# Attention on one Trainium2 core: another order of score and maxima tiles within two steps

## The chip, the cores and the metric

The kernel runs on one core of one Trainium2 chip. TensorE (PE in the profile) multiplies, VectorE (DVE) and ScalarE (ACT) read the results out of PSUM, GpSimd (POOL) works on SBUF alone, SyncE (SP) and POOL issue most DMAs. The metric is device time in microseconds (us) for one execution, a median of several.

## The reference, cut to what matters

A transformer block with adaptive layer norm: softmax attention over 2048 tokens with 32 heads of 18 features, then a gated feed-forward layer (576 to 4608 and back). The change touches the attention alone.

```python
mod = (_silu(c) @ w_mod).reshape(c.shape[0], 6, 1, -1)
h = _layernorm(x) * (1 + ca) + sa
q, k, v = qkv[0], qkv[1], qkv[2]                 # B=1, S=2048, D=576, H=32, Dh=18
scores = jnp.einsum("bhqd,bhkd->bhqk", q, k) * scale
p = _softmax(scores, axis=-1)
o = jnp.einsum("bhqk,bhkd->bhqd", p, v)
x = x + ga * (o @ wo)
h = _layernorm(x) * (1 + cb) + sb
x = x + gb * ((_sigmoid(h @ w_gate) * (h @ w_up)) @ w_down)
```

## The kernel before, in words

Attention is cut into 32 units `u`: a half of the queries (1024) and a pair of heads. A unit has 16 steps `kt`, one for each 128 keys. A step computes four **score tiles** (letter `t`, L1055): 128 keys by 512 queries, for the two heads `h` and the two query chunks `c`. ACT turns each into probabilities with an exponential (L1059, tiles `p0` to `p3`). Two steps later these are multiplied with the values (`values`, L629) and summed in one PSUM tile `o`, which collects a whole unit.

The exponential needs the maximum of each row of scores. So beside unit `u` the maxima for a later unit are found: a step also computes four **maxima tiles** (letter `m`, L524, generator `maxima`), 128 queries by 512 keys, in the order of the table `MAXIMA` or `MAXIMA_H`. DVE reduces seven of eight of them (L530; the one with `h == 0, kc == 1` in L535, together with `over`). The eighth (`h == 0, kc == 0`) is read by ACT, which writes it to `over` (L533); `over` has one buffer.

Scores and maxima use only half of TensorE's rows (56 and 54 of 128): head 0 the upper half, head 1 the lower one. So two neighbouring products of different heads run beside each other as a **pair**. The values product takes four column groups at once.

Every product of either kind, and every transpose, takes the next of seven PSUM banks in turn (`bank()`, tiles `s0` to `s6`). A product can start only when the reader of the seventh allocation before it is done.

Two steps, an even and an odd one, make a **double step**. The order within it is written out by hand as a string for each, and TensorE and ACT keep that order (manual schedule). In most double steps ("halved") the values of the odd step are split in two calls of 256 columns. I call the full call `v`, the two halves `a` and `b`, and number the 16 products of a halved double step 0 to 15. The other letters place the work that comes once in a while:

- `s` and `c`: the maxima of a unit are turned into rows: a transpose on TensorE (L555, in `spread`), a copy on ACT (L559) and a subtraction on DVE (L560). It happens at `kt` 12 of a unit.
- `k` (`taken`): at the end of a unit ACT copies the finished `o` to `oT` (L646). `o` has one buffer, so the next unit's first `v` waits for that copy. It happens at `kt` 1 of the next unit, behind `b`.
- `w` and `c` at `kt` 3 (`outputs`): four transposes of `oT` (L656) into one bank, a reciprocal on DVE (L661), a copy on ACT (L672) that frees the bank.

From step 240 on, rows of the output projection and of the second layer norm (transposes L743, L760, L886, products L776) come in as well, and double steps with L776 aren't halved.

Of the kernel before, what the change touches and what calls it, by code (L numbers as in the profile page):

```python
# [47 lines left out]

MAXIMA = ((1, 0), (0, 0), (1, 1), (0, 2), (1, 2), (0, 3), (0, 1), (1, 3))
SINGLE = (0, 1)  # L50
MAXIMA_H = ((1, 0), (0, 0), (1, 1), (0, 2), (0, 3), (1, 2), (0, 1), (1, 3))
SIDES_H = ((1, 0), (1, 1), (0, 1), (0, 0))
SIDES = ((0, 0), (0, 1), (1, 0), (1, 1))
ORDERED = 7
SEVENS = NB - 2
# [6 lines left out]
def tile_block(ctx, tc, x_in, wqkv, wo, w_gate, w_up, w_down, c_in, w_mod, out):  # L62
# [26 lines left out]
    def bank():  # L89

        turns["bank"] += 1
        return ps[turns["bank"] % 7].tile([P, 512], F32, name=f"s{turns['bank'] % 7}")
# [281 lines left out]
    with tc.tile_pool(name="ln", bufs=2) as ln:  # L374
# [31 lines left out]
        order = ExitStack()  # L406
# [68 lines left out]
    def heads(u):  # L475
        return qsets[u % 3], ksets[u if u < 2 else 2 + (u - 2) % 3]

    def load_heads(u):


        qs, ks = heads(u)
        half, p = divmod(u, H // 2)
        n = S if u < 2 else S + 512
        own = slice(half * HW, (half + 1) * HW)
        for h in range(2):
            rows = slice((2 * p + h) * DH, (2 * p + h + 1) * DH)
            two, one = (slice(64 * h + a, 64 * h + b) for a, b in ((0, 2 * DH), (2 * DH, 3 * DH)))
            nc.sync.dma_start(
                qs[two, :].bitcast(F32), qd[:, rows, own].rearrange("l f n -> f l n").bitcast(F32)
            )  # L490
            nc.sync.dma_start(qs[one, :].bitcast(F32), qd[0, rows, own].bitcast(F32))
            nc.sync.dma_start(
                ks[two, 0:n].bitcast(F32),
                kd[0, rows, 0:n].unsqueeze(1).to_broadcast([DH, 2, n]).bitcast(F32),
            )
            nc.sync.dma_start(ks[one, 0:n].bitcast(F32), kd[1, rows, 0:n].bitcast(F32))
# [3 lines left out]
    def maxima():  # L500
# [4 lines left out]
        for u in range(UNITS):  # L505
# [4 lines left out]
            for i in range(8 * n):  # L510
# [7 lines left out]
                pairs = u not in SINGLE  # L518
                h, kc = (MAXIMA_H if state.get("halved") else MAXIMA)[i % 8]
                rows = slice(64 * h, 64 * h + 3 * DH)  # L520
# [30 lines left out]
    def spread(qs, nm):  # L551

        n = HW // P
        tp = bank()[0 : 2 * n, 0:P]
        nc.tensor.transpose(tp, nm.rearrange("p h t -> p (h t)"), ident)  # L555
        yield
        mrows = small.tile([32 + 2 * n, P], F32R, name="mrows", bufs=1)
        parts = [mrows[32 * l : 32 * l + 2 * n] for l in range(2)]
        nc.scalar.copy(parts[0], tp)  # L559
        nc.vector.tensor_sub(parts[1], tp, parts[0].bitcast(F32))  # L560
        for h in range(2):
            for l, part in enumerate(parts):
                to = 64 * h + 3 * DH + l
                nc.sync.dma_start(
                    qs[to : to + 1, :].rearrange("l (t q) -> l t q", q=P).bitcast(F32),
                    part[n * h : n * (h + 1), :].bitcast(F32),
                )
# [4 lines left out]
    def turn():  # L572
        if turns["s"] < turns["to"]:
            turns["s"] += 1
            next(todo, None)
# [65 lines left out]
    def taken():  # L641

        if "whole" in state:
            half, p, acc = state.pop("whole")
            oT = epool.tile([P, 512], F32, name="oT")
            nc.scalar.copy(oT, acc)  # L646
            state["end"] = (half, p, oT)
# [350 lines left out]
    def load_x(n, name=None):  # L998
        if name:
            X[n] = slots.tile([P, 5, 512], F32R, name=name)  # L1000
        nc.gpsimd.dma_start(X[n], xs[0, n])
# [8 lines left out]
    for u in range(UNITS):  # L1010
        half, p = divmod(u, H // 2)
        qs, ks = heads(u)
        if 0 < u < UNITS - 2:
            load_heads(u + 2)
        if u == H // 2:
            Os.append(big.tile([P, 8, 640], F32, name="big"))
        for kt in range(NT):
            step = u * NT + kt
            turns["to"] = 64 + 4 * LEAD + 4 * (step + 1)
            kcols = slice(kt * P, (kt + 1) * P)  # L1020
            if kt % 2 == 0:
                heavy = state.get("next") == "g"
                hold = heavy and (kt == 2 or kt == 12 and u < UNITS - 1)
                state["halved"] = step >= 10 and (hold or not heavy)
            halved = state["halved"]
            sides = iter(SIDES_H if halved else SIDES)
            probs = [None] * 4
            order = ("vmmtmmtsactt", "wmcmbkttmtmt") if halved else ("vtmmttmvtm", "ktmwttmctmm")
            for does in order[kt % 2]:
                if does == "m":  # L1030
                    turn()
                elif does == "k":
                    taken()
                elif does in "ws":
                    if kt == 3:
                        follow.append(outputs())
                        next(follow[-1], None)
                    if "spread" in state and halved == (does == "s"):
                        follow.append(spread(*state.pop("spread")))
                        next(follow[-1])  # L1040
                    if step >= FROM0 and not hold and halved == (does == "s"):
                        state["next"] = next(rows0 if step < FROM1 else rows1, None)
                elif does == "c":
                    while follow:
                        next(follow.pop(0), None)
                elif does == "v":
                    if step >= LAG:
                        values()
                elif does in "ab":
                    values(slice(0, 256) if does == "a" else slice(256, 512))  # L1050
                else:
                    c, h = next(sides)
                    sT = bank()
                    rows = slice(64 * h, 64 * h + 3 * DH + 2)
                    nc.tensor.matmul(  # L1055
                        sT, ks[rows, kcols], qs[rows, c * 512 : (c + 1) * 512], start=True, stop=True
                    )
                    pr = probs[2 * c + h] = ppool.tile([P, 512], F32, name=f"p{2 * c + h}")
                    state["exp"] = nc.scalar.activation(pr, sT, AF.Exp, scale=SCALE)  # L1059
            pending.append((half, p, kt, probs))  # L1060
            if u in (1, 3):
                if kt == 0:
                    a = big.tile([P, 8, 640], F32, name="big")
                    a = a.rearrange("p a b -> p (a b)")[:, 0 : 8 * D].rearrange("p (t c) -> p t c", t=4)
                    b = slots.tile([P, 2560], F32, name="w0")[:, 0 : 2 * D]
                    mods = load_mod(a, b, 1 + u // 2)
                    row = slots.tile([P, 2560], F32, name="w1")[:, 0:544]
                    weighed = weigh(mods)
                elif kt >= 5:
                    next(weighed, None)  # L1070
            elif u in (2, 4) and kt in (2, 4):
                takes = [(ga_b, None), (mcol2[:, 1, :], 0.0)] if u == 2 else [(mcol2[:, 0, :], 1.0), (gb_b, None)]
                if kt == 2:
                    weighed = modulate(row, mods[:1], HALVES, takes)
                next(weighed, None)
            if 4 * NT + 8 <= step < FROM0 and step % 4 != 3:
                next(downs, None)
            if step == FROM0:
                for _ in downs:
                    pass  # L1080
            if step == FROM1 - 1:
                for _ in rows0:
                    pass
                bgs.close()
                rawst = ExitStack()
                raws = rawst.enter_context(tc.tile_pool(name="raws", bufs=1, side="right"))
            if u == 30 and kt == 7:
                first = [load_block(raws, b, k, paced) for b, k in ((0, 0), (0, 1), (1, 1))]
            if u >= 30 and kt == 2:
                load_x(u - 30, f"k{u - 30}")  # L1090
            if u == UNITS - 1 and kt == 3:
                nc.sync.dma_start(oend[:, :, 0 : D - DL - 2 * DH], Os[1][:, :, DL : D - 2 * DH])
            if u == UNITS - 1 and kt == 9:
                for _ in rows1:
                    pass
                load_x(2, "w0")
                load_x(3, "w1")
                both = big.tile([P, 2, 5, 512], F32R, name="big")
                for i in range(2):
                    X[5 + i] = both[:, i]  # L1100
                    load_x(5 + i)
# [687 lines left out]
```

## Time and profile before

| what | value |
|---|---|
| time, median of 3 runs | 2802.93 us (2802.58 to 2807.48) |
| span of the profiled execution | 2801.3 us |
| TensorE busy | 2766.6 us (99%) |
| VectorE busy | 2302.7 us (82%) |
| ScalarE busy | 1607.0 us (57%) |
| exponentials (L1059) on ACT | 1078.1 us, 2048 of 621 ns |
| row maxima (L530) on DVE | 993.8 us, 1568 of 683 ns |
| granted TensorE clock, mean | 0.999 |

The profiled execution has no time of its own beside its span; the median of the runs is 1.6 us above that span. A busy PE is not PE at its peak: the ends of matmuls are modelled, and a product that waits for its bank can hide under the modelled end of the one before it. So the times between the starts of PE's rows say more than its busy share. Attention fills the stretch from about 240 to 1530 us.

### The profile page before, as it was taken

How to read it: one execution, taken by the hardware profiler on the slowest of the kernel's cores; microseconds unless marked ns; L12 is line 12 of the kernel's file. 1: busy time of each engine (PE TensorE's matmuls, PEld its weight loads, DVE VectorE, ACT ScalarE, POOL GpSimd, SP SyncE). 2: the span in 40 equal slices, each digit the busy share in tenths (PEclk: the TensorE clock that was granted, in tenths of full speed). 3: DMA queues.
4: the chain of work that ended last, by engine and by line, in shares of the span. 5: the costliest groups of instructions: out<-in, count | busy, mean ns of one | idle time of the engine just before them, and what ended most of it. 6: DMA issues, size and time to landing. Idle time of an engine off the chain costs nothing.

```text
span 2801.3 us, 50850 instructions
## 1 busy us (share of the span) xinstructions
PE 2766.6 (99%) x18637; PEld 1830.4 (65%) x18637; DVE 2302.7 (82%) x4370; ACT 1607.0 (57%) x3051; POOL 816.2 (29%) x1077
## 2 busy tenths in 40 slices
PE   7999999999999999999999999999999999999999
PEld 5975444444444444444444888888888888888888
DVE  7278999999998888999883788888898677777777
ACT  3216999999999778999888322333333222222221
POOL 3125208887843111663113222222221100000000
PEclk9999999999999999999999999999999999999999
DMA  5344215444442120232126766667767966666663
GB/s 173 123 155 147 72 59 173 168 173 157 170 135 80 36 59 24 98 106 71 43 68 219 266 220 228 232 217 266 279 249 274 355 201 196 203 196 200 199 197 120
DMA packets 170778, 462.60 MB, mean 165 GB/s; under 512 B 21212, under 2 KB 88032, under 8 KB 160416
## 3 DMA queue, kind: packets, MB, share of 16 engines
q1 hardware_dynamic: 150064, 360.72, 38.7%
q0 software_dynamic: 20464, 98.62, 10.0%
q8 instruction: 147, 2.41, 0.4%
q14 instruction: 103, 0.84, 0.1%
HBM read 281.92 MB, written 176.82 MB: 164 GB/s over the span
## 4 chain that ended last, share of the span: by engine, by line
PE 93%; DVE 4%; issue 1%; DMA 1%; ACT 1%; POOL 0%; SPq 0%; DVEq 0%; ACTq 0%; POOLq 0%
PE x L1196 28%; PE o L629 19%; PE s L1055 12%; PE s L524 10%; PE d L1346 8%; PE d L1278 6%; PE s L310 4%; PE s L776 2%; PE s L363 1%; DVE mx L530 1%; PE s L656 1%; ACT p L1059 1%; DMA wq_raw<-in_A_wqkv_dram 0%; DVE Oa L1350 0%; DVE w L1186 0%
## 5 line engine op out<-in xcount | busy, mean ns | idle before, releaser
L1059 ACT ACTIVATE p<-s 128x512 f32<-128x512 f32 x2048 | 1078.1, 621 | 98.8 <-PE s L1055 83.5
L530 DVE TENSOR_REDUCE mx<-s 128x1 f32<-128x512 f32 x1568 | 993.8, 683 | 108.0 <-PE s L524 93.3
L629 PE MATMUL o<-p,vaug 128*32 128x256 f32 (+1 forms) x5848 | 592.4, 477 | 3.1 <-ACT p L1059 2.5
L1055 PE MATMUL s<-q,k 56*128 56x512 f32 x1920 | 516.6, 449 | 0.0
L524 PE MATMUL s<-k,q 54*128 54x512 f32 x1920 | 501.3, 427 | 2.6 <-DVE t L746 1.7
L524 PEld LDWEIGHTS s<-k,q 54*128 54x128 f32 x1920 | 275.6, 185 | 231.6 <-DVE mx L535 161.0
L1055 PEld LDWEIGHTS s<-q,k 56*128 56x128 f32 x1920 | 246.9, 184 | 242.7 <-issue 112.8
L1196 PE MATMUL x<-k,w 128*128 128x512 f32 x1512 | 368.6, 391 | 0.0
L1196 PEld LDWEIGHTS x<-k,w 128*128 128x128 f32 x1512 | 276.9, 188 | 53.1 <-issue 1.7
L629 PEld LDWEIGHTS o<-p,vaug 128*32 128x32 f32 x5848 | 115.4, 108 | 209.7 <-issue 130.7
L1346 PE MATMUL d<-wd,hh 128*128 128x288 f32 x1248 | 249.9, 295 | 2.4 <-DVE Oa L1350 2.4
L1196 PE MATMUL x<-big,w 128*128 128x512 f32 x1008 | 244.9, 391 | 2.1 <-DVE u L1690 1.4
L1196 PE MATMUL x<-w,w 128*128 128x512 f32 x1008 | 245.1, 391 | 0.0
L1196 PEld LDWEIGHTS x<-big,w 128*128 128x128 f32 x1008 | 185.1, 188 | 38.5 <-DVE u L1690 2.3
L1196 PEld LDWEIGHTS x<-w,w 128*128 128x128 f32 x1008 | 184.4, 188 | 34.3
L1346 PEld LDWEIGHTS d<-wd,hh 128*128 128x128 f32 x1248 | 202.2, 188 | 6.2 <-DVE Oa L1350 3.1
L1346 PE MATMUL d<-wd,hl 128*128 128x288 f32 x624 | 184.3, 295 | 0.0
L1350 DVE TENSOR_TENSOR Oa<-Oa,d 128x288 f32<-128x288 f32 x312 | 136.4, 452 | 54.8 <-PE d L1346 50.8
L535 DVE CUSTOM_DVE_ANT_0 over<-s,over 128x512 f32<-128x512 f32 x240 | 164.4, 685 | 0.7 <-ACT p L1059 0.3
L533 ACT ACTIVATE over<-s 128x512 f32<-128x512 f32 x240 | 150.1, 626 | 7.4 <-PE s L524 7.3
L1205 ACT ACTIVATE sg<-x 128x512 f32<-128x512 f32 x36 | 21.6, 599 | 207.8 <-PE x L1196 207.8
L1177 ACT CAST w<-S 128x768 fp32r<-128x768 f32 x71 | 59.4, 836 | 137.5 <-POOL S L1150 135.6
(274 smaller groups left out, 3889.8 us busy)
## 6 DMA issues: line engine op xcount, KB each, us to landing
ws<-w SPq DMA_DIRECT2D x126, 640.0 KB
w<-ws SPq DMA_DIRECT2D x126, 640.0 KB
wd<-wds SPq DMA_DIRECT2D x19, 1152.0 KB
k<-kd SPq DMA_DIRECT2D x60, 360.0 KB
wds<-w POOLq DMA_DIRECT2D x18, 1152.0 KB, 5.6
wtd<-t POOLq DMA_DIRECT2D x32, 576.0 KB, 4.8
wt<-wtd SPq DMA_DIRECT2D x64, 288.0 KB
wd<-wds SPq DMA_DIRECT2D x52, 288.0 KB
```

The source lines that it names most:

```text
L310: nc.tensor.matmul(acc, w, hT[:, t, cols], start=n == 0, stop=n == len(ts_) - 1)
L524: nc.tensor.matmul(sp, qs[rows, qt * P : (qt + 1) * P], ks[rows, at * 512 : (at + 1) * 512], start=True, stop=True,)
L530: nc.vector.tensor_reduce(to, sp, axis=AX.X, op=ALU.max)
L533: nc.scalar.activation(over, sp, AF.Relu)
L535: nc.vector.tensor_tensor_reduce(out=over, in0=sp, in1=over, scale=1.0, scalar=LOWEST, op0=ALU.add, op1=ALU.max, accum_out=mx[:, h * n + q ...
L629: nc.tensor.matmul(acc[32 * j : 32 * j + 32, cols], vaug[:, kt, (2 * p + h) * VW : (2 * p + h) * VW + 32], probs[2 * c + h][:, cols], star ...
L1055: nc.tensor.matmul(sT, ks[rows, kcols], qs[rows, c * 512 : (c + 1) * 512], start=True, stop=True)
L1059: state["exp"] = nc.scalar.activation(pr, sT, AF.Exp, scale=SCALE)
L1196: nc.tensor.matmul(acc[v], w[:, v, a, :], X[s][:, b, :], start=first and n == 0, stop=n == 6, skip_group_check=not first,)
L1278: nc.tensor.matmul(acc, a[:, rows], w[:, k, :], start=n == 0, stop=n == 2)
L1346: nc.tensor.matmul(acc[:, :HALF], a[:, f, rows], w[:, f, cols], start=n == 0, stop=n == 5)
L1350: nc.vector.tensor_add(Oa[:, t, cols], Oa[:, t, cols], acc[:, :HALF])
```

## The change

The table of maxima for halved double steps, the order of the score tiles in them (now one order for even steps and one for odd ones), and the two order strings of a halved double step are other ones. No instruction is added or taken away, and steps that aren't halved keep their order.

```diff
-MAXIMA_H = ((1, 0), (0, 0), (1, 1), (0, 2), (0, 3), (1, 2), (0, 1), (1, 3))
-SIDES_H = ((1, 0), (1, 1), (0, 1), (0, 0))
+MAXIMA_H = ((1, 0), (0, 2), (1, 1), (0, 0), (1, 2), (0, 3), (1, 3), (0, 1))
+SIDES_H = (((0, 0), (1, 0), (0, 1), (1, 1)), ((0, 0), (0, 1), (1, 0), (1, 1)))
...
-            sides = iter(SIDES_H if halved else SIDES)
+            sides = iter(SIDES_H[kt % 2] if halved else SIDES)
...
-            order = ("vmmtmmtsactt", "wmcmbkttmtmt") if halved else ("vtmmttmvtm", "ktmwttmctmm")
+            order = ("vmtttmmsacmt", "wmtcbktmmttm") if halved else ("vtmmttmvtm", "ktmwttmctmm")
```

Written out with the product numbers (m* is the maxima tile that ACT reads; a small letter stands where that work comes in):

```
before  v 0m 1m* 2t 3m 4m 5t (s) a (c) 6t 7t (w) 8m (c) 9m  b (k) 10t 11t 12m 13t 14m 15t
after   v 0m 1t  2t 3t 4m 5m (s) a (c) 6m* 7t (w) 8m 9t (c) b (k) 10t 11m 12m 13t 14t 15m
```

So ACT reads 1, 2, 5, 6, 7, 10, 11, 13 and 15 before, and 1, 2, 3, 6, 7, 9, 10, 13 and 14 now; DVE reads the rest. Of the eight pairs (0 1), (2 3) and so on, four held a score and a maxima tile before, and six do now.

What moves on the engines is shown at three places. The first is ACT around the copy of a finished unit (L646; the tenth of the program). `s0` to `s6` are the banks, `p0` to `p3` the probabilities, `over` the maxima tile that ACT reads. Before:

```order
L1059 ACTIVATE p3_8448<-s4_8446 128x512
L1059 ACTIVATE p1_8456<-s5_8454 128x512
L1059 ACTIVATE p0_8460<-s6_8458 128x512
L646 COPY oT_8477<-o_7866 128x512
L1059 ACTIVATE p2_8481<-s2_8479 128x512
L1059 ACTIVATE p3_8485<-s3_8483 128x512
```

and now:

```order
L1059 ACTIVATE p1_8442<-s2_8440 128x512
L533 ACTIVATE over_8456<-s5_8454 128x512
L1059 ACTIVATE p3_8460<-s6_8458 128x512
L1059 ACTIVATE p0_8472<-s1_8470 128x512
L646 COPY oT_8478<-o_7866 128x512
L1059 ACTIVATE p1_8482<-s2_8480 128x512
```

Between `a` and the copy ACT had the products 6 and 7 (banks `s5`, `s6`) to read, and now has 6, 7 and 9 (`s5`, `s6`, `s1`): the copy has moved back by one activation.

The second place is TensorE in the double step in which a unit's maxima are spread (the eleventh L555), from product 3 to product 9. Before:

```order
L524 MATMUL s4_8270<-k0_2230,q2_1029 128x512
L524 MATMUL s5_8273<-k0_2230,q2_1029 128x512
L1055 MATMUL s6_8276<-q0_1025,k1_2233 128x512
L555 MATMUL s0_8280<-ident_84,nm_8171 16x128
L629 MATMUL o_7866<-p0_8253,vaug_117 32x256
L629 MATMUL o_7866<-p2_8235,vaug_117 32x256
L629 MATMUL o_7866<-p1_8246,vaug_117 32x256
L629 MATMUL o_7866<-p3_8239,vaug_117 32x256
L1055 MATMUL s1_8293<-q0_1025,k1_2233 128x512
L1055 MATMUL s2_8297<-q0_1025,k1_2233 128x512
L524 MATMUL s3_8306<-k0_2230,q2_1029 128x512
L524 MATMUL s4_8309<-k0_2230,q2_1029 128x512
```

and now:

```order
L1055 MATMUL s4_8270<-q0_1025,k1_2233 128x512
L524 MATMUL s5_8274<-k0_2230,q2_1029 128x512
L524 MATMUL s6_8277<-k0_2230,q2_1029 128x512
L555 MATMUL s0_8280<-ident_84,nm_8175 16x128
L629 MATMUL o_7866<-p0_8228,vaug_117 32x256
L629 MATMUL o_7866<-p2_8246,vaug_117 32x256
L629 MATMUL o_7866<-p1_8236,vaug_117 32x256
L629 MATMUL o_7866<-p3_8250,vaug_117 32x256
L524 MATMUL s1_8293<-k0_2230,q2_1029 128x512
L1055 MATMUL s2_8297<-q0_1025,k1_2233 128x512
L524 MATMUL s3_8306<-k0_2230,q2_1029 128x512
L1055 MATMUL s4_8309<-q0_1025,k1_2233 128x512
```

The transpose takes a bank of its own, so product 9 gets the bank of product 3 (`s4`). That was a maxima tile, which DVE reads, and is now the third score tile in a row, which ACT reads.

The third place is TensorE between `b` and the next `v`, products 10 to 15 of the double step with that copy. Before:

```order
L1055 MATMUL s2_8479<-q1_1021,k2_2236 128x512
L1055 MATMUL s3_8483<-q1_1021,k2_2236 128x512
L524 MATMUL s4_8487<-k0_2230,q2_1029 128x512
L1055 MATMUL s5_8490<-q1_1021,k2_2236 128x512
L524 MATMUL s6_8494<-k0_2230,q2_1029 128x512
L1055 MATMUL s0_8497<-q1_1021,k2_2236 128x512
```

and now:

```order
L1055 MATMUL s2_8480<-q1_1021,k2_2236 128x512
L524 MATMUL s3_8484<-k0_2230,q2_1029 128x512
L524 MATMUL s4_8487<-k0_2230,q2_1029 128x512
L1055 MATMUL s5_8490<-q1_1021,k2_2236 128x512
L1055 MATMUL s6_8494<-q1_1021,k2_2236 128x512
L524 MATMUL s0_8498<-k0_2230,q2_1029 128x512
```

The number of products between the two calls is the same. Four score tiles and two maxima tiles have become three and three, since product 9, ahead of `b`, is now a score tile; the last product before `v` is now one that DVE reads.

## Rows read from the trace of the kernel before

**Rows 1.** One stretch of attention: length, busy PE, PEld, DVE, ACT, POOL; clock; DMA.

```profile
600.00:700.00 100.00, 100.00 (x847) 41.13 (x851) 92.45 (x176) 96.86 (x197) 83.73 (x135) 1.00 0.45 163
```

**Rows 2.** Groups of instructions, from the page: busy, mean ns, idle before.

```profile
L1059 ACT ACTIVATE p<-s 128x512 f32<-128x512 f32 x2048 | 1078.1, 621 | 98.8 <-PE s L1055 83.5
L629 PE MATMUL o<-p,vaug 128*32 128x256 f32 (+1 forms) x5848 | 592.4, 477 | 3.1 <-ACT p L1059 2.5
```

**Rows 3.** PE in order of time, a unit's last double step: start, length, what.

```profile
620.17 0.50 PE L1055 MATMUL s<-q,k 56*128 56x512 f32 x2
...
621.09 1.07 PE L629 MATMUL o<-p,vaug 128*32 128x512 f32 x8
622.08 0.73 PE L524 MATMUL s<-k,q 54*128 54x512 f32 x3
622.42 0.39 PE L1055 MATMUL s<-q,k 56*128 56x512 f32 x1
622.65 0.39 PE L524 MATMUL s<-k,q 54*128 54x512 f32 x1
...
622.98 0.64 PE L629 MATMUL o<-p,vaug 128*32 128x256 f32 x8
623.89 0.46 PE L524 MATMUL s<-k,q 54*128 54x512 f32 x2
624.28 0.64 PE L629 MATMUL o<-p,vaug 128*32 128x256 f32 x8
624.85 0.50 PE L1055 MATMUL s<-q,k 56*128 56x512 f32 x2
...
625.42 0.40 PE L524 MATMUL s<-k,q 54*128 54x512 f32 x1
...
625.81 1.07 PE L629 MATMUL o<-p,vaug 128*32 128x512 f32 x8
```

**Rows 4.** ACT in order of time, the same stretch and the double step behind it.

```profile
620.76 2.07 ACT L1059 ACTIVATE p<-s 128x512 f32<-128x512 f32 x4 [0.16 <-PE s L1055]
622.69 0.63 ACT L533 ACTIVATE over<-s 128x512 f32<-128x512 f32 x1
623.16 2.11 ACT L1059 ACTIVATE p<-s 128x512 f32<-128x512 f32 x4
625.12 0.64 ACT L646 COPY oT<-o 128x512 f32<-128x512 f32 x1
...
630.16 0.59 ACT L672 COPY oT<-s 128x512 f32<-128x512 f32 x1
```

**Rows 5.** What waited for the copy of a finished unit (L646): us, times.

```profile
  PEld o L629: 8.6, 27
```

**Rows 6.** PE in the double step with a unit's outputs.

```profile
627.78 0.64 PE L629 MATMUL o<-p,vaug 128*32 128x256 f32 x8
...
629.36 0.50 PE L524 MATMUL s<-k,q 54*128 54x512 f32 x2
629.79 0.64 PE L629 MATMUL o<-p,vaug 128*32 128x256 f32 x8
...
631.27 1.07 PE L629 MATMUL o<-p,vaug 128*32 128x512 f32 x8
```

**Rows 7.** The copy of the outputs (L672): count, min/median/max ns, first and last.

```profile
L672 ACT COPY oT<-s x31: 586/736/747, 281.6 to 1503.7; 128x512 f32<-128x512 f32 x31
```

**Rows 8.** PE in the double step in which maxima are spread.

```profile
611.52 1.06 PE L629 MATMUL o<-p,vaug 128*32 128x512 f32 x8
...
613.64 0.64 PE L629 MATMUL o<-p,vaug 128*32 128x256 f32 x8
...
614.87 0.64 PE L629 MATMUL o<-p,vaug 128*32 128x256 f32 x8
...
616.45 1.07 PE L629 MATMUL o<-p,vaug 128*32 128x512 f32 x8
```

**Rows 9.** What waited for the subtraction of the spread (L560): us, times.

```profile
  PEld s L1055: 11.1, 27
```

## The prediction

> **What bounds the kernel now.** I first read the busy times of a stretch of attention. In 100 us PE is busy all the time, ACT for 96.86 us and DVE for 92.45 us, at full clock (1.00) [rows 1]. So three engines are near their limit, and it must be found out which one waits for which. Next I counted. A call of `values` leaves 8 rows (x8 in [rows 3]), and all calls leave 5848 [rows 2]; that is 731 calls for 512 steps, so 219 steps have two calls: 219 halved double steps, the only place that the change touches.
>
> Then I read PE in order of time, by the starts of its rows [rows 3]. Here v is the time of the full call, A that of the first half call. From v to the first product 0.99 us pass (621.09 to 622.08), from the first pair to the second 0.34, to the third 0.23, and from the last pair to the next call 0.33 (622.65 to 622.98). From a half call to the first product it is 0.57 (624.28 to 624.85). With these gaps alone a double step would take 1.89 to `a`, 0.57 + 0.34 + 0.33 = 1.24 to `b`, and 0.57 + 0.34 + 0.23 + 0.33 = 1.47 to the next v: 4.60 us. The one shown takes 4.72 us (621.09 to 625.81): `a` to `b` 1.30, `b` to v 1.53.
>
> ACT in the same stretch says why [rows 4]. It is idle once, for 0.16 us, and then starts at 620.76, 0.59 us after the product at 620.17 that it waits for. Five activations later, at 623.16, it reads the tile whose bank product 9 needs: 2.40 us, 0.48 for each. That exponential lasts about 0.63 us, as its neighbour at 622.69 does; then product 9 can start (its pair is the row at 623.89), and `b` comes at 624.28, 0.49 after the exponential's end. 0.57 later comes the first product behind `b`, and 0.59 after that ACT begins the next round. 2.40 + 0.63 + 0.49 + 0.57 + 0.59 = 4.68 us: a ring through ACT and PE, 0.08 longer than PE alone would take. It is this ring, not PE's work, that sets the pace of a quiet double step.
>
> **The change, part by part.** *Quiet double steps.* In the new order the first product behind `a` is 6, and ACT is ready for it. It has read 1, 2 and 3 from v + 0.99 + 0.59 = v + 1.58 on, in 3 times 0.48, so it is free at v + 3.02; product 6 can be read at A + 0.57 + 0.59 = A + 1.16, which is v + 3.05 or later. So ACT's idle time now lies there. Then it reads 6, 7, 9, 10, 13 and 14: the last starts 2.40 us later, ends 0.63 after that at A + 4.19, and frees the bank of product 5 of the next double step (seven allocations on). `a` follows 0.49 later: A + 4.68. It is the same ring with the same members, entered at `a` instead of `b`. I take 0 for it. The bounds: nothing better than PE's own 4.60, so -0.08 times 219 = -17.5 us; and if the bank of product 14, which waits for the reading of 7, is late as well, some 0.05 more in each of the 134 double steps that are left when the three kinds below are taken off: +7 us.
>
> The Trainium skill, page TensorEngine Tiling (Array Packing), section "PSUM Bottleneck", says that reading PSUM can become the limit when small products run side by side, and that both ScalarE and VectorE should share it. The new order does that within nearly every pair, and by the rule the waits for banks should shrink. By [rows 1] both readers were already near full, and what each reads in a double step stays the same, nine and seven tiles; the rule would make the lower bound above the sum, the ring makes it zero.
>
> *The copy of a finished unit (L646), which the next unit's first v waits for.* Before, ACT reads 6 and 7 behind A and then copies: the copy starts at 625.12, A + 2.14, ends at 625.76, and v stands at 625.81 [rows 3, 4]. Without the copy v could have come at 624.28 + 1.47 = 625.75, so the copy was hidden but for 0.06. Now ACT has 6, 7 and 9 ahead of it, and starts 6 at A + 1.16: the copy starts at A + 1.16 + 3 x 0.49 = A + 2.63, lasts 0.64, and v comes 0.05 later, at A + 3.32. It was at A + 2.83. So 0.49 us more, and nothing covers it: PE has nothing else to start. 27 units paid that wait before [rows 5]; 27 x 0.49 = +13.2 us. The bounds: nothing, if ACT were ahead by one activation; and 0.57 each, if `a` to `b` also loses its wait of 0.06, which I count once only in the ring.
>
> *The copy of a unit's outputs (L672), which frees the bank of the four transposes.* With A the half call at 627.78, product 9 starts at about 629.36, A + 1.58 [rows 6], and ACT can read it at A + 2.17, end it at A + 2.77, and end the copy 0.48 later, at A + 3.25. That bank is needed by product 14 in the third pair behind `b`; with the 0.49 from a free bank to the call behind its pair, v comes at A + 3.74. It was at 631.27, A + 3.49, with the copy ended at 630.75 [rows 4], in time for the third pair. So 0.25 more. Against that, v was late just before, ACT has caught up, and the wait of 1.97 - 1.89 = 0.08 between 625.81 and 627.78 [rows 3, 6] goes. 0.17 net, and 31 of these copies [rows 7] make +5.3 us.
>
> *The spread of the maxima.* The transpose takes a bank, so product 9 now waits for the reading of product 3. ACT reads 1, 2, 3 from v + 1.58; the third ends at v + 1.58 + 0.96 + 0.63 = v + 3.17, and `b` follows 0.49 later, at v + 3.66. It was at 614.87, v + 3.35 [rows 8]: 0.31 more. Behind `b` the old order lost 1.58 - 1.47 = 0.11 (614.87 to 616.45), waiting for the subtraction; that bank's product now comes later, and the wait is hidden. 0.20 net; 27 double steps waited there before [rows 9], so +5.4 us.
>
> What else moves costs nothing: ACT's reading of the maxima tile and DVE's use of `over` stand further apart than before, no DMA, no POOL work and no double step without halves moves.
>
> The sum is 13.2 + 5.3 + 5.4 = 23.9 us on the span of 2801.3, so 2825.2. The median of the runs lies 1.6 above the span: 2826.8. From step 240 on other transposes stand in some of these double steps and lengthen them, so a few of the 85 prices will not be paid in full; I take 1 us off and say **2826**, 0.8% slower.
>
> **The rivals.**
>
> *Faster.* The mixed pairs break the ring: if ACT is ready for product 6 without a wait, because it runs a little ahead, product 5 finds its bank free and each double step falls to 4.60. All 219 would give -17.5, so 2785; with the three terms above still paid it is 2809, slower. To end below 2797 the quiet steps must gain nearly all, and the copy must start by A + 2.07 (v's free place at A + 2.71 + 0.05 less 0.64 and 0.05), so less than two activations after 6. Against it: ACT cannot read 6 before A + 1.16, and three activations follow. This is the way that the Trainium skill's rule on sharing the reading of PSUM (the page and section above) would have it.
>
> *No change.* The ring stays, and the three delays find cover. That needs an activation to be done in well under 0.48, which no row of ACT shows; or ACT's order not to be kept, against the order in the program. 2803.
>
> *Slower, by the finished unit alone.* The copy of the outputs and the spread are hidden by the time that the late v gives ACT: 2803 + 13 = 2816.
>
> *Slower still.* The ring gets longer by the second wait in each quiet double step (product 14 behind 7): 2826 + 7 = 2833, and some 2 more if the finished unit costs 0.57.
>
> **How the numbers follow.** The forecast, 2818 to 2831, has a chance of 0.55; the finished unit alone 0.16; slower still 0.15; no change 0.08; faster 0.06. A measurement of this kernel can tell about 0.2%, 5.6 us, from no change. So slower holds 0.86, same 0.08, faster 0.06. The range reaches down into the case of one term, with a gain of some us in the ring, to 2810, and up to 2837.
>
> **What would show it.** Right: in the double step with L646 the time from `a` to the v behind it is near 3.3 us (before 2.83), and the wait of the values' weights for that copy grows from 0.32 us each [rows 5] by about half a us; behind the outputs `a` to v is 3.7; in a spread v to `b` is 3.6; quiet double steps stay at 4.68; the clock stays at 1.00. Wrong: if quiet double steps come out at 4.60 the ring isn't what I think, and if v does not wait longer for L646, ACT had room that the rows hide.

## The result, and the profile after

The changed kernel takes 2818.75 us (median of 4 runs, 2817.34 to 2819.77) against 2803.01 us of the kernel before on the same chip (2802.58 to 2807.48): ratio 1.0047, 95% interval 1.0033 to 1.0061. It is slower, by 15.7 us; forecast were 23.

The page of the profiled execution after, first line and busy times:

```profile
span 2816.3 us, 50270 instructions
...
PE 2774.8 (99%) x18637; PEld 1846.8 (66%) x18637; DVE 2311.8 (82%) x4370; ACT 1613.8 (57%) x3051; POOL 815.9 (29%) x1077
```

The same 100 us of attention as in [rows 1]:

```profile
600.00:700.00 100.00, 99.13 (x843) 42.05 (x841) 92.07 (x174) 96.01 (x194) 78.17 (x125) 1.00 0.48 172
```

The clock is full, DVE and ACT have each a little less to do per microsecond, and PE, which was never idle, now is for 0.87 us of 100. So the added time is waiting. Where it lies is read from the starts of the half calls, as in [rows 3]. A **turn** below is the double step with the copy L646, an **out** that with the outputs, a **spread** that with L555, and **quiet** is the rest. PE in a turn (v 549.22, `a` 551.18, `b` 552.42, next v 554.39), and ACT beside it:

```profile
549.22 1.06 PE L629 MATMUL o<-p,vaug 128*32 128x512 f32 x8
...
551.18 0.64 PE L629 MATMUL o<-p,vaug 128*32 128x256 f32 x8
551.75 0.50 PE L524 MATMUL s<-k,q 54*128 54x512 f32 x1
...
552.42 0.64 PE L629 MATMUL o<-p,vaug 128*32 128x256 f32 x8
...
554.39 1.06 PE L629 MATMUL o<-p,vaug 128*32 128x512 f32 x8 [0.43 <-ACT oT L646]
```

```profile
552.28 0.60 ACT L533 ACTIVATE over<-s 128x512 f32<-128x512 f32 x1
552.78 1.08 ACT L1059 ACTIVATE p<-s 128x512 f32<-128x512 f32 x2
553.73 0.60 ACT L646 COPY oT<-o 128x512 f32<-128x512 f32 x1
```

From `a` to v 3.21 us pass, where 2.83 passed before [rows 3]. ACT reads products 6, 7 and 9 first (552.28, then two), and the copy ends at 554.33, 0.06 ahead of v. What waited for L646, and the outputs of the same unit (`a`, `b`, v; L672 on ACT):

```profile
  PEld o L629: 21.2, 28
  PE o L629: 11.7, 27
```

```profile
556.30 0.64 PE L629 MATMUL o<-p,vaug 128*32 128x256 f32 x8
...
558.33 0.64 PE L629 MATMUL o<-p,vaug 128*32 128x256 f32 x8
...
560.02 1.06 PE L629 MATMUL o<-p,vaug 128*32 128x512 f32 x8
```

```profile
558.96 0.58 ACT L672 COPY oT<-s 128x512 f32<-128x512 f32 x1
```

The weights of v wait 0.76 us each for the copy, against 0.32 [rows 5]. The second line is the same wait, seen on the call: PE itself stands still for 0.43 of it. Behind the outputs `a` to v is 3.72 (before 3.49, [rows 6]), and `b` to v 1.69. A spread, v to `b` 3.63 (before 3.35, [rows 8]):

```profile
539.52 1.07 PE L629 MATMUL o<-p,vaug 128*32 128x512 f32 x8
...
541.65 0.64 PE L629 MATMUL o<-p,vaug 128*32 128x256 f32 x8
...
543.15 0.64 PE L629 MATMUL o<-p,vaug 128*32 128x256 f32 x8
...
544.62 0.64 PE L629 MATMUL o<-p,vaug 128*32 128x512 f32 x4
```

And a quiet one, PE and the row in which ACT comes out of its pause:

```profile
525.60 1.07 PE L629 MATMUL o<-p,vaug 128*32 128x512 f32 x8
...
527.55 0.64 PE L629 MATMUL o<-p,vaug 128*32 128x256 f32 x8
528.12 0.49 PE L524 MATMUL s<-k,q 54*128 54x512 f32 x1
...
528.79 0.64 PE L629 MATMUL o<-p,vaug 128*32 128x256 f32 x8
...
530.25 1.06 PE L629 MATMUL o<-p,vaug 128*32 128x512 f32 x8
```

```profile
528.65 0.60 ACT L533 ACTIVATE over<-s 128x512 f32<-128x512 f32 x1
```

That is 4.65 us, a little less than before. All halved double steps that could be followed whole in both traces (212 of 219, some lack records) give this, in us, the first columns being medians:

```
                        v to a         a to b         b to v         together       sum of all
kind             count  before after   before after   before after   before after   after - before
turn                22   1.90   1.95    1.29   1.23    1.53   1.98    4.71   5.16     +9.9
turn with rows       5                                                5.30   5.69     +1.5
out                 24   1.97   1.91    2.02   2.02    1.47   1.69    5.45   5.62     +4.3
out with rows        6                                                6.09   6.31     +1.4
spread              27   2.10   2.13    1.24   1.48    1.60   1.47    4.93   5.09     +2.5
spread with rows     3                                                5.37   5.29     -0.2
quiet              104   1.89   1.93    1.31   1.23    1.48   1.47    4.69   4.64     -4.0
quiet with rows     21                                                5.22   5.22     +1.1
```

("With rows": products of the output projection's rows or of the second layer norm stand among them. The medians of quiet are of the 62 that don't follow an out or a spread.) The sum is +16.5; all of attention, with the double steps that aren't halved, is 15.3 us longer (from the first start of L629 to the last, 1295.7 before and 1311.0 after), and the span 15.0.

### The profile page after: what moved, and what is told of

It is laid out like the page before. It is cut to its first block, busy times and chain, and to the rows that moved or that the text cites. A ratio compares the mean times of both kernels' runs of the same rounds, so it can differ in the third digit from the quotient of the medians.

```text
span 2816.3 us, 50270 instructions
## 1 busy us (share of the span) xinstructions
PE 2774.8 (99%) x18637; PEld 1846.8 (66%) x18637; DVE 2311.8 (82%) x4370; ACT 1613.8 (57%) x3051; POOL 815.9 (29%) x1077
## 4 chain that ended last, share of the span: by engine, by line
PE 90%; DVE 4%; ACT 2%; DMA 2%; issue 2%; SPq 0%; POOL 0%; DVEq 0%; POOLq 0%; ACTq 0%
PE x L1196 27%; PE o L629 18%; PE s L524 12%; PE s L1055 10%; PE d L1346 8%; PE d L1278 6%; PE s L310 4%; PE s L776 2%; ACT p L1059 2%; PE s L363 1%; DVE mx L530 1%; PE s L656 1%; DMA wq_raw<-in_A_wqkv_dram 1%; ACT oT L646 0%; DVE Oa L1350 0%
## 5 line engine op out<-in xcount | busy, mean ns | idle before, releaser
L1059 ACT ACTIVATE p<-s 128x512 f32<-128x512 f32 x2048 | 1075.5, 612 | 101.6 <-PE s L1055 68.2
L524 PE MATMUL s<-k,q 54*128 54x512 f32 x1920 | 637.1, 436 | 1.6 <-DVE t L746 1.6
L629 PE MATMUL o<-p,vaug 128*32 128x256 f32 (+1 forms) x5848 | 593.1, 477 | 11.7 <-ACT oT L646 11.7
L1055 PE MATMUL s<-q,k 56*128 56x512 f32 x1920 | 600.9, 440 | 0.4 <-ACT oT L672 0.3
L524 PEld LDWEIGHTS s<-k,q 54*128 54x128 f32 x1920 | 298.9, 184 | 285.7 <-ACT p L1059 117.9
L1055 PEld LDWEIGHTS s<-q,k 56*128 56x128 f32 x1920 | 267.1, 184 | 193.8 <-ACT over L533 47.8
L629 PEld LDWEIGHTS o<-p,vaug 128*32 128x32 f32 x5848 | 115.8, 108 | 212.8 <-issue 184.1
L533 ACT ACTIVATE over<-s 128x512 f32<-128x512 f32 x240 | 144.7, 603 | 14.3 <-PE s L1055 10.6
```

The lines of the kernel that those rows point to most:

```text
L524: nc.tensor.matmul(sp, qs[rows, qt * P : (qt + 1) * P], ks[rows, at * 512 : (at + 1) * 512], start=True, stop=True,)
L533: nc.scalar.activation(over, sp, AF.Relu)
L629: nc.tensor.matmul(acc[32 * j : 32 * j + 32, cols], vaug[:, kt, (2 * p + h) * VW : (2 * p + h) * VW + 32], probs[2 * c + h][:, cols], star ...
L1055: nc.tensor.matmul(sT, ks[rows, kcols], qs[rows, c * 512 : (c + 1) * 512], start=True, stop=True)
```

## The experiments

All were timed against the kernel before in 5 rounds, on the same chip as that one, so runs are compared by their ratios (the kernel after has 1.0047); a number such as "turn 5.16" is the median length of that kind of double step, from the same reading as in the table.

**x1_copy_before_9: the copy one activation earlier.** In a turn the exponential of product 9 is issued behind the copy (its code stands a few lines lower: scores are L1062 and exponentials L1031 there).

```diff
+            late = []
+
+            def read(pr, sT):
+                state["exp"] = nc.scalar.activation(pr, sT, AF.Exp, scale=SCALE)
...
                 elif does == "k":
                     taken()
+                    if late:
+                        read(*late.pop())
...
-                    state["exp"] = nc.scalar.activation(pr, sT, AF.Exp, scale=SCALE)
+                    if halved and kt == 1 and sum(x is not None for x in probs) == 1:
+                        late.append((pr, sT))
+                    else:
+                        read(pr, sT)
```

> The new order, with ACT's copy of a finished unit (L646) put ahead of its reading of product 9; TensorE keeps its order. Theory V (as the prediction has it: v waits for the copy, and the copy stands one activation too late): the 0.45 us of the 27 double steps with the copy come back, 27 x 0.45 = 12 us, so about 2807 against 2819 for the new order. Theory R (the ring: ACT reads 6, 7, 9, 10, 13, 14 without a pause and the next product 5 waits for the last of them; a tenth activation in that row costs 0.48 us wherever it stands): v comes early again, a to v 2.8 to 2.85, but the next stretch from v to a grows from 1.91 to about 2.35; about 2817 to 2820.

Measured: 2820.49 us, ratio 1.0047 (1.0035 to 1.0060), the same as after. ACT and PE in a turn and behind it:

```profile
552.31 0.59 ACT L646 COPY oT<-o 128x512 f32<-128x512 f32 x1
```

```profile
550.24 0.64 PE L629 MATMUL o<-p,vaug 128*32 128x256 f32 x8
...
551.47 0.64 PE L629 MATMUL o<-p,vaug 128*32 128x256 f32 x8
...
552.96 1.07 PE L629 MATMUL o<-p,vaug 128*32 128x512 f32 x8
...
555.35 0.64 PE L629 MATMUL o<-p,vaug 128*32 128x256 f32 x8
```

The copy starts at A + 2.07 and v is on time, 1.49 behind `b` (after: 1.98) and 2.72 behind `a`, even a little ahead of what was expected. But the next `a` comes 2.39 behind v instead of 1.91: the turn falls from 5.16 to 4.67, the out behind it grows from 5.62 to 6.10. What v no longer waits, `a` does. So the price isn't that of the copy's place ahead of v.

**x2_c_before_9: the second half of the outputs (`c`: L661, L672) ahead of product 9.**

```diff
-            order = ("vmtttmmsacmt", "wmtcbktmmttm") if halved else ("vtmmttmvtm", "ktmwttmctmm")
+            order = ("vmtttmmsacmt", "wmctbktmmttm") if halved else ("vtmmttmvtm", "ktmwttmctmm")
```

> The new order, with the letter c one place earlier in the odd step (ahead of product 9), so that ACT copies a unit's outputs (L672) before it reads product 9. The prediction's reason (the bank of the transposes is freed too late for product 14): a to v in the double step with the outputs falls from 3.70 to about 3.5, 31 x 0.18 = 5 to 6 us back, so about 2813. The rival (an extra activation in the row costs the same wherever it stands): no gain, 2818 to 2820.

Measured: 2814.19 us, ratio 1.0029 (1.0018 to 1.0041). PE in an out:

```profile
557.70 0.64 PE L629 MATMUL o<-p,vaug 128*32 128x256 f32 x8
...
559.72 0.64 PE L629 MATMUL o<-p,vaug 128*32 128x256 f32 x8
...
561.18 0.64 PE L629 MATMUL o<-p,vaug 128*32 128x512 f32 x4
```

`b` to v is 1.46 instead of 1.69, and the median of outs 5.40 instead of 5.62. In after, weights of score tiles waited for L672 30 times, 12.6 us in all; here none do. The row of after:

```profile
  PEld s L1055: 12.6, 30
```

So the bank that L672 frees, needed by product 14, was this wait.

**x3_exp_first_behind_a: a score tile as product 6 and m* as product 7.** ACT now leaves its pause with an exponential.

```diff
-            order = ("vmtttmmsacmt", "wmtcbktmmttm") if halved else ("vtmmttmvtm", "ktmwttmctmm")
+            order = ("vmtttmmsactm", "wmtcbktmmttm") if halved else ("vtmmttmvtm", "ktmwttmctmm")
```

> The new order with products 6 and 7 changed about: behind a ACT reads a score tile first and the maxima tile second. All pairs hold the same two tiles. Theory E (the quiet double step got 0.04 us shorter because ACT, after its pause, now begins with the reading of a maxima tile, which starts 0.53 us after its product, where the exponential before started 0.59 after its own): quiet double steps go back up by 0.04 to 0.06, 104 of them and some others, so +4 to +6 us, 2823 to 2825. Theory P (they got shorter because the pairs are mixed): no change, 2818 to 2820.

Measured: 2826.08 us, ratio 1.0072 (1.0059 to 1.0084), one us above what was expected (its trace has the stretch at a lower clock that is told of at x8). PE in a quiet double step (v, product 6, next v), and ACT's reading of product 6, 0.59 behind it:

```profile
569.76 1.07 PE L629 MATMUL o<-p,vaug 128*32 128x512 f32 x8
...
572.29 0.49 PE L1055 MATMUL s<-q,k 56*128 56x512 f32 x1
...
574.45 1.06 PE L629 MATMUL o<-p,vaug 128*32 128x512 f32 x8
```

```profile
572.88 0.60 ACT L1059 ACTIVATE p<-s 128x512 f32<-128x512 f32 x1
```

Turns get 0.06 longer too (5.22). Quiet double steps go from 4.640 to 4.686 us, which is their length before (4.685), with six mixed pairs as in after. So the 4 us that quiet double steps gained hang on which activation comes first, not on the mixed pairs.

**x4_dve_third: all eight pairs mixed.** Products 3 and 4 change places, so that product 3, whose bank product 9 of a spread gets, is read by DVE.

```diff
-SIDES_H = (((0, 0), (1, 0), (0, 1), (1, 1)), ((0, 0), (0, 1), (1, 0), (1, 1)))
+SIDES_H = (((0, 0), (0, 1), (1, 0), (1, 1)), ((0, 0), (0, 1), (1, 0), (1, 1)))
...
-            order = ("vmtttmmsacmt", "wmtcbktmmttm") if halved else ("vtmmttmvtm", "ktmwttmctmm")
+            order = ("vmttmtmsacmt", "wmtcbktmmttm") if halved else ("vtmmttmvtm", "ktmwttmctmm")
```

> The new order with products 3 and 4 changed about, and the heads of the score tiles of even steps in the order of odd steps: product 3 is a maxima tile again, which DVE reads, and all eight pairs hold one of each kind. The bank theory of the spread (product 9 waits for ACT's reading of product 3 there): v to b in those double steps falls from 3.62 to about 3.4, and 27 x 0.16 = 4 us come back, 2815. If the spread's price comes from its copy on ACT (L559) instead: no gain, 2819. If mixed pairs by themselves help (theory P), quiet double steps get shorter again, by 0.02 to 0.04, another 2 to 4 us: 2811 to 2813.

Measured: 2816.21 us, ratio 1.0037 (1.0025 to 1.0050). PE in a spread:

```profile
577.42 1.07 PE L629 MATMUL o<-p,vaug 128*32 128x512 f32 x8
...
580.79 0.64 PE L629 MATMUL o<-p,vaug 128*32 128x256 f32 x8
...
582.34 1.07 PE L629 MATMUL o<-p,vaug 128*32 128x512 f32 x8
```

v to `b` is back at 3.37, the spread's median at 4.93 as before the change (5.09 after). Outs lose 0.06 (5.68). Quiet double steps stay at 4.640. The rule on sharing the reading of PSUM (the Trainium skill, page TensorEngine Tiling (Array Packing), section "PSUM Bottleneck") finds no support here: pairs whose two tiles go to different readers are five of eight before, after and in x3, and seven in x4, and the quiet double step takes 4.685, 4.640, 4.686 and 4.640. (Pairs of a score and a maxima tile are four, six, six and eight; but m* goes to ACT, as the score tiles do.)

**x5_copy_on_dve: the copy L646 on DVE, in the kernel after.**

```diff
-            nc.scalar.copy(oT, acc)
+            nc.vector.tensor_copy(oT, acc)
```

> The kernel after, with the finished unit's copy into oT (L646, kt 1 of the row) given to DVE instead of ACT; nothing else moves. Theory R (in a turn double step ACT reads ten things in the ring instead of nine, and the tenth costs its 0.45 to 0.49 us wherever it stands): the turn's 5.16 us fall back to the quiet 4.64 to 4.70, the out double steps stay near 5.62; about -10 to -13 us, 2806 us, ratio 1.000 to 1.002. Rival D (DVE has no room there: it is busy over nine tenths of the stretch, so the copy only moves the wait to the products of the maxima tiles): the turn stays at 5.0 or above, 2815 us or more.

Measured: 2807.76 us, ratio 1.0009 (1.0001 to 1.0018). DVE and PE in a turn, and what waited for L646:

```profile
552.84 0.69 DVE L646 COPY oT<-o 128x512 f32<-128x512 f32 x1
```

```profile
550.83 0.64 PE L629 MATMUL o<-p,vaug 128*32 128x256 f32 x8
...
552.07 0.64 PE L629 MATMUL o<-p,vaug 128*32 128x256 f32 x8
...
553.59 0.64 PE L629 MATMUL o<-p,vaug 128*32 128x512 f32 x4
```

```profile
  PEld o L629: 9.8, 28
```

The turn is 4.71 us (5.16 with the copy on ACT), the out behind it 5.60. DVE is busy for 93.89 us of 100 here and still has room, for its pause lies there. In after, with the copy on ACT, its row behind the reading of product 8 reads

```profile
553.55 1.29 DVE L530 TENSOR_REDUCE mx<-s 128x1 f32<-128x512 f32 x2 [0.32 <-PE s L524]
```

in a turn in which v comes 3.21 behind `a`; in x5 DVE's next reading starts 0.61 behind the copy's start, so the copy fills those 0.32 us and takes 0.29 more, of which 0.07 show in the turn. Theory R holds, rival D falls.

**x6_before_copy_on_dve: the same edit in the kernel before.**

> The same edit in the kernel before: its copy L646 goes to DVE. There the turn costs only 4.71 us with the copy on ACT, since ACT has a pause at that point and DVE reads products 8 and 9 just ahead of it. Theory R with DVE's reads packed: on DVE the copy stands behind those reads and the half call b or v waits for it, the turn grows by 0.3 to 0.45 us, +8 to +12 us, ratio 1.003 to 1.0045. Rival: DVE has room and the turn stays at 4.70, ratio 1.000; if ACT's pause was worth more, below 0.999.

Measured: 2819.08 us, ratio 1.0053 (1.0041 to 1.0066). DVE and PE in a turn:

```profile
549.30 3.08 DVE L530 TENSOR_REDUCE mx<-s 128x1 f32<-128x512 f32 x5 [0.33 <-PE s L524]
552.30 0.68 DVE L646 COPY oT<-o 128x512 f32<-128x512 f32 x1
```

```profile
550.98 0.64 PE L629 MATMUL o<-p,vaug 128*32 128x256 f32 x8
...
553.04 1.06 PE L629 MATMUL o<-p,vaug 128*32 128x512 f32 x8 [0.52 <-DVE oT L646]
```

In this order DVE's pause of 0.33 lies ahead of the first maxima tile behind v, and then it reads five tiles without a gap; the copy comes at A + 2.62 (in x5 at A + 2.01), and v waits for it: turn 5.27, where 4.71 stood with the copy on ACT. That is a little more than expected (0.55 instead of at most 0.45 each). So one and the same edit gains 11 us in one order (1.0047 to 1.0009) and loses 15 in the other: the copy is nearly free on the engine whose pause lies at the copy's place, ACT in the order before, DVE in the order after.

**x8_two_edits: x2 and x4 together, the copy on ACT.** The order strings are `vmttmtmsacmt` and `wmctbktmmttm`, SIDES_H as in x4.

> The kernel after with the step c earlier and product 3 as DVE's, the copy L646 left on ACT. Added gains of x2 and x4: 2812 to 2814 us, ratio 1.001 to 1.003, the turn still at 5.16. If the two edits interact, at or above x2's 1.003.

Measured: 2807.09 us, ratio 1.0009 (1.0000 to 1.0018): better than expected. Out 5.39, spread 4.93, turn still 5.16; the 0.06 that x4 alone lost in outs doesn't occur with `c` earlier.

An interaction of the two edits isn't shown by this. All 219 halved double steps together take 1093.8 us in the trace of after, 1086.5 in x2, 1089.8 in x4 and 1081.9 here: gains of 7.3, 4.0 and 11.9, which add but for 0.6. By the ratios the gains are 0.0018, 0.0010 and 0.0038, and the 0.0010 between is no more than the interval of each. Besides, the trace of x2 loses 2.6 us ahead of all halved double steps: the stretch from the first L629 to the first of them takes 22.8 us in x2, x3 and x5 and 20.1 or 20.2 in before, after, x4, x7 and x8. Six us of it, the first row of after, the second of x2:

```profile
239.00:245.00 6.00, 6.00 (x42) 2.31 (x36) 6.00 (x11) 4.84 (x10) 3.72 (x5) 1.00 1.02 355
239.00:245.00 6.00, 6.00 (x26) 1.49 (x26) 4.11 (x7) 2.76 (x6) 3.32 (x5) 0.50 1.02 347
```

TensorE's granted clock there is 1.00 (2.4 GHz) in after and 0.50 (1.2 GHz) in x2. In the 8 us ahead of it PE was busy for 7.06 in both, and the order strings that differ come into force only behind it. Why the clock fell in x2, and how many of the executions without a trace had it, isn't known.

**x7_three_edits: x8 and the copy on DVE.**

> The kernel after with three edits together: the copy L646 on DVE (as in x5), the step c between products 8 and 9 (as in x2, which took the out double steps from 5.62 to 5.40), and the score tile (0,1) and the maxima tile (0,1) swapped so that product 3 is DVE's (as in x4, which took the spread double steps from 5.09 to 4.93). If the three gains are of different places they add: -12, -5 and -2.5 us on the kernel after, about 2799 us, ratio 0.9965 to 0.9995, a little faster than both kernels. Rival: one of them takes another's room (DVE's copy behind a DVE read that now stands earlier), then no better than x5 alone, ratio 1.000 to 1.002.

Measured: 2795.16 us, ratio 0.9969 (0.9957 to 0.9981), faster than both kernels (0.3% under the one before). Turn 4.70, out 5.39, spread 4.93, quiet 4.64: what the new order lost is gone, and the shorter quiet double step stays. The ratio is as expected, and the gains add: all halved double steps take 1070.2 us, 23.6 less than in after, where x5 (12.0), x2 and x4 make 23.3 (1077.6 in before).

## Why the prediction was right, and where it was off

**The bound.** That waits of PE for banks set the pace, and not PE's work, held: in after PE's products are the same and its idle time rises. The ring was right too. With the entry from the rows of after (551.75 to 552.28 is 0.53) its members are 0.57 + 0.53 + 2.40 + 0.63 + 0.49 = 4.62; measured are 4.64. What the prediction says of sharing the reading "within nearly every pair" is wrong for this change: counted by the engine that reads, five of eight pairs are shared before and five after (x4).

**Quiet double steps: forecast 0, measured -4.0 us.** The step that failed is "the same ring with the same members". One member is another: ACT comes out of its pause with m* (L533) 0.53 us after the product, where the exponential of the order before took 0.59 [rows 3, 4] (the last section tells what goes with it; that this is its cause isn't shown). x3 puts an exponential there again and gets 4.686 back. It lay within the bounds that were given, but its sign was not weighed. The wait of product 14 for the reading of 7, the other bound, didn't come.

**The copy of a finished unit: forecast +13.2, measured +11.4** (9.9 and 1.5). `a` to v was forecast at 3.32 and is 3.21: ACT's entry is 0.06 earlier, and the copy, at A + 2.55, ends sooner after its start. The price was right, the reason not wholly. The prediction put the loss on v, which waits for that copy, and held that it would go if the copy started by A + 2.07. In x1 it starts exactly there, and the time doesn't move. The reading that x5 and x6 bear out: in the order after, the copy stands inside ACT's row from product 6 to 14, which closes the ring, so its 0.48 is added to the ring, at either of the two places tried. In the order before, the row begins behind the copy, with product 10, which could be read from 624.85 + 0.59 = 625.44 on; the copy was begun at 625.12, and 0.48 later ACT was free again, 0.16 late only [rows 3, 4].

**The copy of the outputs: forecast +5.3, measured +5.7** (4.3 and 1.4). `a` to v was forecast at 3.74 and is 3.72, and the wait ahead of `a` went as said (1.97 to 1.91). x2 shows that the bank of product 14 is the cause.

**The spread: forecast +5.4, measured +2.4.** The mechanism ahead of `b` is the one foretold: v to `b` 3.63 (forecast 3.66), and x4 takes the price away by giving product 3 to DVE. Behind `b` the 0.11 of the old order are gone (`b` to v 1.47), but they weren't the wait for the subtraction that the prediction took them for. The 11.1 us of [rows 9] are 0.41 for each of 27, and in after the same wait stands 29 times:

```profile
  PEld s L1055: 11.9, 29
```

Yet nothing is lost behind `b` in after; in x4 it is there 3 times only, and `b` to v is 1.57. What made the 0.11 stays open. The term was also mis-sized: the row used [rows 8] gave 0.20, the medians 0.16; and where other work already lengthens the double step (one of 27 was 1 us shorter after, and the three with rows 0.2 in all), it isn't paid.

**The sum.** Forecast on the span +23 (23.9, less 1), measured +15.0, so the time lies at the lower end of the range (2818 to 2831). Of the missing 8, quiet double steps are 4.0, spreads 3.0 and the finished unit 1.8, outs were 0.4 too low; the rest, in quiet double steps with rows, in those not halved and in the 1 taken off, comes to about 0.5 the other way. Of the rivals "finished unit alone" gave 2816 and would have been nearer in number, but by another way: its two other terms are there, and the gain in quiet double steps offsets most of them.

What else stays open: why outs get 0.06 longer in x4, and not when `c` comes earlier (x8), was read from their lengths alone, and not tried apart.

## What to carry to other kernels

Where two engines hand tiles round in a ring, find the place at which the reading engine pauses in each round: here work that comes once in a while was nearly free there, and cost most of its time at the other places tried (two on ACT, one on DVE). When an order moves the pause, move that work too, or give it to the engine that now pauses there; the share of busy time (92 to 94% of DVE, in x5 and in x6 alike) doesn't tell whether it fits. And before moving a piece of work earlier to end a wait, ask who stands behind it: x1 moved a wait of 0.48 us from one call to the next and won nothing.

## What the runs showed of the hardware

How long ACT takes, behind a pause, from a product's start to the start of its reading differs with whether a wait is an instruction of its own. Between 300 and 850 us of the trace before, 126 exponentials behind a pause have a semaphore instruction of their own just ahead and start a median of 0.593 us after the product; 14 have none and start after 0.536. After the change the pause ends with m* (L533), without such an instruction: 42 of them, median 0.534. In x3, 103 exponentials with one again take 0.593. All these products are the first of their pair (6 and 10). The place in the pair counts too: 112 exponentials of product 1, the second of its pair, have no such instruction in after and start after 0.563. In the whole program such instructions became fewer with the change, on L1059 from 1171 to 616 and on L533 from 239 to 31:

```profile
L533 ACTq EVENT_SEMAPHORE  x31: 17/17/17, 888.6 to 1487.4; - x31
```

```profile
L1059 ACTq EVENT_SEMAPHORE  x616: 17/17/296, 234.8 to 1547.5; - x154
```

That instruction shows as 17 ns, and 0.06 us go with it. It is a difference between cases, not an edit of that instruction alone; in a ring the 0.06 count in every round.
